# Loading and turning the first inputs of a fused attention and ELU-FFN kernel in another layout, with one block of M made early

## The chip, the cores and the metric

The kernel runs on one core of a Trainium2 chip. The metric is the device time of one execution in microseconds; a kernel's time is the median over its runs.

## The reference

`x` is (8, 8, 512, 64): batch B, heads H, tokens S, width D. `state` is (8, 8, 32, 64). Everything is fp32.

```python
scores = x @ state^T / 8;   xread = softmax(scores) @ state      # per batch and head, 512 x 32
scores2 = state @ x^T / 8;  sread = softmax(scores2) @ x         # 32 x 512
t = concat([xread, sread], axis=2)                               # 544 tokens per batch
t = t.transpose(0, 2, 1, 3).reshape(4352, 512)                   # heads side by side
h = t @ w_in                                                     # 512 -> 2048
g = where(h > 0, h, exp(min(h, 0)) - 1)
out = g @ w_out                                                  # 2048 -> 512
```

## The kernel before

**Algebra.** For the x part, xread @ w_in is a @ (state @ w_in): the kernel makes M = blockdiag(state) @ w_in for each batch (256 rows: 8 heads x 32 states) and multiplies the turned softmax `aT` with it (`ffn1_plain`, `ffn1_chunk`). w_in is cut into eight column blocks `hc` of 256; `make_m(b, hc)` makes one block of M with small products in PE tiles of 64 x 32 (`by_state`), and ACT copies it from PSUM. The 256 state tokens of all batches are read (`state_read`) batch by batch and put through the FFN at the end (`states`). Batches 2 to 7 use Strassen-Winograd sums for both FFN products, batches 0 and 1 for the second.

**Weights.** `convert` brings each weight block into another bit form with two ACT and four DVE passes. The eight w_in blocks and eight w_out blocks pass through three raw buffers (`t_w`), so block n + 3 is loaded when block n has been converted. A converted w_in block is also stored to DRAM (`w_in_mem`), and from batch 2 on `fetch(hc)` brings it back, 512 KB each.

**Stages.** `start()` does batches 0 and 1 together with the conversion of the weights: x of batch 0 is loaded and turned (`load_x`, `turn_x`), then scores, `softmax`, one block of M after another, FFN products as each is ready, the row softmax and the state read; then the w_out blocks and the second product. x of batch 0 lies in `xe` (`x_halves`), that of batch 1 in `g` (`x_1`). Then `ffn2_1` for batch 1 and `batch(b)` for 2 to 7, in which the first blocks of M of the next batch (`first_m`, `next_m`) and its softmax lie between the products of the running one; there x is loaded a second time in a blocked form and turned by DVE (`load_blocks`, `turn_blocks`), and the row softmax is brought in place by 16 small moves on SP's queue (`move_state`).

**Order.** Every operation is recorded in a `Plan` first. `ORDERS` holds one list of operation numbers for each engine, written out; `Plan.follow` walks through them with estimated costs (`DMA_COST`, `LAG`, `LANDING`), and by these picks PSUM banks, the interleaving in which instructions are emitted, and where PE gets fillers: products of the identity into a free bank while PE would wait, in the first 40 us of the plan. Nothing of the estimates acts on the chip but these choices. SP's queue issues nearly all transfers in its written order. All of this goes through helpers, so that in the profile nearly everything has line L525; fillers are L1675. Tiles tell the operations apart: `ps<-sec,xe` turns x of batch 0, `ps<-sec,g` that of batch 1, `ps<-o,kT` are the scores of batches 0 and 1, `ps<-w_half,kT` blocks of M, `ps<-aT,m` and `ps<-s,g` the first FFN products of batches 0 and 1, `ps<-xe,xr` a state read; `w_half<-t_w` and `t_w<-t_w` on ACT, `w_half` and `t_w` on DVE are conversions.

Of the kernel before, what the change touches and what calls it, by code (L numbers as in the profile page):

```python
# [11 lines left out]
FP32 = mybir.dt.float32  # L12
# [10 lines left out]
    "load_w": (0.44, 285e3), "load_w4": (0.44, 370e3), "load_x": (0.6, 270e3), "load_states": (0.6, 75e3),  # L23
    "load_blocks": (0.66, 280e3, 1.5), "move_state": (0.66, 280e3),
    "store": (0.44, 200e3), "store_q": (0.44, 90e3),
# [15 lines left out]
def in_order(text):  # L41

    ops = []
    for part in text.split():
# [40 lines left out]
    ),  # L85
    DVE: in_order(
# [152 lines left out]
class Plan:  # L239
# [6 lines left out]
        ACT: {PE: 0.23, DVE: 0.14, ACT: 0.12, POOL: 0.18, SP: 0.2},  # L246
        POOL: {PE: 0.12, DVE: 0.08, ACT: 0.08, POOL: 0.1, SP: 0.2},
    }
    LANDING = 2.2
    TURN = 0.1  # L250
    KEPT_BANKS = 0

# [107 lines left out]
    def follow(self, orders, until=0.0):  # L360
# [14 lines left out]
        def choice(op):  # L375
            if op.number < self.all_banks:
                return banks
# [1339 lines left out]
```

## Time and profile before

| | |
|---|---|
| time, median of 3 runs | 692.6 us (692.35 to 692.69) |
| span of the profiled execution | 689.9 us |
| outside the span, against the median | 2.7 us |
| PE busy (fillers included) | 683.8 us |
| DVE / ACT / GpSimd busy | 571.6 / 328.5 / 107.9 us |
| fillers on PE (L1675) up to 46 us | 16.7 us, 120 matmuls |
| bytes moved | 78.56 MB, of 111400 packets 89188 under 512 B |

The span runs from the first to the last instruction. An fp32 product is two matmuls in the trace, a transpose is one. "PEld" is the weight load of PE, which lies beside the matmuls. The durations of neighbouring matmuls overlap, so a step from start to start is the better measure of what one costs. A busy engine is not always doing needed work: fillers count as busy.

### The profile page before, as it was taken

How to read it: one execution, taken by the hardware profiler on the slowest of the kernel's cores; microseconds unless marked ns; L12 is line 12 of the kernel's file. 1: busy time of each engine (PE TensorE's matmuls, PEld its weight loads, DVE VectorE, ACT ScalarE, POOL GpSimd, SP SyncE). 2: the span in 40 equal slices, each digit the busy share in tenths (PEclk: the TensorE clock that was granted, in tenths of full speed). 3: DMA queues.
4: the chain of work that ended last, by engine and by line, in shares of the span. 5: the costliest groups of instructions: out<-in, count | busy, mean ns of one | idle time of the engine just before them, and what ended most of it. 6: DMA issues, size and time to landing. Idle time of an engine off the chain costs nothing.

```text
span 689.9 us, 14828 instructions
## 1 busy us (share of the span) xinstructions
PE 683.8 (99%) x5968; PEld 593.6 (86%) x5968; DVE 571.6 (83%) x897; ACT 328.5 (48%) x728; POOL 107.9 (16%) x133
## 2 busy tenths in 40 slices
PE   9999999999999999999999999999999999999997
PEld 7544568889988998899989998899889998999996
DVE  3999999989859994999679976998599966988661
ACT  4899973201268233842286316822383328611530
POOL 0200000110141115111240132212330333000000
PEclk9999999999999999999999999999999999999999
DMA  9767972003772237440383035232634030330401
GB/s 241 233 214 258 265 199 73 2 0 109 212 180 76 68 91 196 98 124 1 120 214 106 22 118 125 96 109 63 190 69 133 22 123 3 104 111 1 153 1 31
DMA packets 111400, 78.56 MB, mean 114 GB/s; under 512 B 89188, under 2 KB 92900, under 8 KB 111332
## 3 DMA queue, kind: packets, MB, share of 16 engines
q1 hardware_dynamic: 109120, 77.06, 39.1%
q8 instruction: 47, 0.77, 0.4%
q10 hardware_dynamic: 2212, 0.56, 0.4%
q14 instruction: 21, 0.17, 0.1%
HBM read 61.34 MB, written 13.11 MB: 108 GB/s over the span
## 4 chain that ended last, share of the span: by engine, by line
PE 96%; DVE 1%; ACT 1%; POOL 0%; issue 0%; POOLq 0%
PE ps L525 94%; PE ps L1675 2%; DVE sec L525 1%; ACT sec L525 0%; ACT o L525 0%; ACT w_half L525 0%; POOL sec L525 0%; ACT t_w L525 0%; ACT xr L525 0%; DVE s L525 0%; DVE w_half L525 0%; ACT g L525 0%; POOL sec masks.py:199 0%; DVE o L525 0%; ACT m L525 0%
## 5 line engine op out<-in xcount | busy, mean ns | idle before, releaser
L525 ACT COPY ps<-ps 128x128 f32<-128x128 f32 (+2 forms) x169 | 54.9, 331 | 228.2 <-PE ps L525 193.0
L525 PE MATMUL ps<-aT,m 128*128 128x256 f32 (+1 forms) x568 | 150.7, 406 | 0.1
L525 PEld LDWEIGHTS ps<-aT,m 128*128 128x128 f32 x568 | 104.3, 190 | 29.2 <-issue 11.6
L525 PE MATMUL ps<-w_out,g 128*128 128x128 f32 (+1 forms) x768 | 117.2, 293 | 0.0
L525 PEld LDWEIGHTS ps<-w_out,g 128*128 128x128 f32 x768 | 102.8, 192 | 6.6 <-issue 1.8
L525 DVE TENSOR_TENSOR o<-o,ps 128x256 f32<-128x256 f32 (+2 forms) x108 | 56.7, 533 | 38.1 <-PE ps L525 29.7
L525 POOL TENSOR_TENSOR m<-m 128x256 f32<-128x256 f32 x72 | 56.8, 807 | 134.4 <-ACT m L525 74.8
L525 PE MATMUL ps<-sec 128*128 128x128 f32 x560 | 72.7, 275 | 0.0
L525 POOL TENSOR_TENSOR xr<-xr,small 128x512 f32<-128x512 f32 x24 | 29.2, 1232 | 267.0 <-DVE small L525 146.9
L525 PE MATMUL ps<-t_w,s 128*128 128x128 f32 (+1 forms) x432 | 69.3, 299 | 0.0
L525 PEld LDWEIGHTS ps<-sec 128*128 128x128 f32 x560 | 67.7, 192 | 1.4 <-ACT ps L525 0.8
L525 PEld LDWEIGHTS ps<-t_w,s 128*128 128x128 f32 x432 | 59.0, 191 | 4.7 <-DVE sec L525 0.8
L525 ACT ACTIVATE xe<-ps 128x512 f32<-128x512 f32 x96 | 56.2, 599 | 11.5 <-PE ps L525 5.6
L525 DVE SCALAR_TENSOR_TENSOR g<-xe,ps 128x512 f32<-128x512 f32 x66 | 44.2, 681 | 6.8 <-ACT xe L525 6.4
L525 DVE TENSOR_TENSOR ps<-sec,ps 128x512 f32<-128x512 f32 (+1 forms) x52 | 34.8, 671 | 11.0 <-PE ps L525 7.1
L525 ACT COPY m<-ps 128x512 f32<-128x512 f32 (+1 forms) x56 | 29.2, 529 | 27.0 <-PE ps L525 27.0
L525 ACT ACTIVATE xe<-xe 128x512 f32<-128x512 f32 x66 | 41.1, 635 | 1.1
L525 PE MATMUL ps<-aT,s 128*128 128x256 f32 x168 | 41.2, 379 | 0.0
L525 ACT COPY sec<-ps 128x512 f32<-128x512 f32 (+1 forms) x52 | 29.6, 570 | 22.0 <-PE ps L525 21.8
L525 PE MATMUL ps<-w_out,sec 128*128 128x256 f32 (+1 forms) x176 | 38.5, 351 | 0.0
L525 PE MATMUL ps<-sec,g 128*128 128x128 f32 (+1 forms) x300 | 36.9, 270 | 0.0
L525 PEld LDWEIGHTS ps<-aT,s 128*128 128x128 f32 x168 | 31.9, 190 | 4.3
(148 smaller groups left out, 1165.9 us busy)
## 6 DMA issues: line engine op xcount, KB each, us to landing
w_half<-w_in_mem SPq DMA_DIRECT2D x54, 512.0 KB
t_w<-in_moe_w_out_dram SPq DMA_DIRECT2D x8, 1024.0 KB
t_w<-in_moe_w_in_dram SPq DMA_DIRECT2D x7, 1024.0 KB
out_dram<-o SPq DMA_DIRECT2D x14, 512.0 KB
xe<-in_x_dram SPq DMA_DIRECT2D x26, 256.0 KB
o<-in_x_dram SPq DMA_DIRECT2D x80, 64.0 KB
w_in_mem<-w_half SPq DMA_DIRECT2D x8, 512.0 KB
xr<-xr SPq DMA_DIRECT2D x96, 32.0 KB
```

Source lines behind the costliest of these rows:

```text
L525: ins = getattr(engine, name)(**named)
L1675: nc.tensor.matmul(psum[:, i, part * 256 : part * 256 + P], ident, rhs, start=not part, stop=True, skip_group_check=True,)
```

## The change

- `load_x` brings x of a batch in four DMAs by pairs of heads, in runs of 256 elements (1 KB: four tokens of a head), where it went in four DMAs by token residue in runs of 64 (256 bytes). All eight batches use it.
- `turn_x` turns x of batches 0 and 1 by products: each 64 x 64 block is the stationary operand and a 64 x 64 identity the moving one, in four PE tiles of 64 x 64. It took transposes of 64 x 128 blocks.
- The states come in four DMAs of 128 KB (two batches each, on 32 partitions) and are turned at the start, where 16 DMAs of 32 KB brought them, 12 of these later.
- In the first queues x of batch 0 leads, then the states of batches 0 and 1, then w_in's block 0, x of batch 1, the other states, blocks 1 and 2. It was block 0, state, x of batch 0, block 1, x of batch 1.
- `early_m` makes block 0 of M for batches 2 to 7 in the first weight step, into w_out's still unused space, and stores it in DRAM (`m_mem`). `first_m` then fetches that 256 KB block and makes one block (`make_one`) where it fetched 512 KB of w_in and made two.
- `load_blocks(2)` stands earlier in SP's order. In `start`, `y` takes any free bank. The estimates of the plan differ, fillers are spaced otherwise (21 are left of 60), and all five orders are new. Code lines move by 7 and more: helpers are L532, fillers L1731.

```diff
-    def load_x(b, to, queues=(SP,)):
-        x_v = x[b].rearrange("h (p r) d -> p r h d", r=R)
-        for r in range(R):
-            dma(x_rows(to, r).rearrange("p (h d) -> p h d", d=D), x_v[:, r], ...)
+        x_v = x[b].rearrange("(m g) (p r) d -> m p g (r d)", g=G, r=R)
+        for m in range(NP):
+            dma(x_pair(to, m).rearrange("p (g q) -> p g q", g=G), x_v[m], ...)
...
     def turn_x(at, to, both=False):
         for i in range(2):
             ps = [bank(), bank()]
-            for m in range(NP):
-                for r in range(2):
-                    calls += turn_calls(
-                        [v[t][:, m, r] for t in range(2)],
-                        x_rows(at, 2 * i + r)[:, m * P : (m + 1) * P],
-                    )
-            turns(0.6, calls, "turn_x")
+            for m in range(2):
+                for r in range(R):
+                    for g in range(G):
+                        for t in range(2):
+                            rows, d = slice(t * 64, (t + 1) * 64), slice(g * D, (g + 1) * D)
+                            calls.append((
+                                v[t][d, m, r], x_rows(at, 2 * i + m, g, r)[rows],
+                                ident[rows, rows],
+                                dict(start=True, stop=True, tile_position=(t * 64, g * D)),
+                            ))
+            products(1.03, calls, "turn_x", "turn_x")
...
+    def load_states(q, raw, queue=SP):
+        dma(
+            raw[q * NS : (q + 1) * NS].rearrange("p (k d) -> p k d", d=D), state_v[q],
+            queue=queue, kind="load_states",
+        )
+    def turn_states(qs, raw):
+        ps = [bank() for q in qs]
+        for k in range(2 * NP):
+            for q, p in zip(qs, ps):
+                rows = slice(q * NS, (q + 1) * NS)
+                calls.append((
+                    p[:, k * NS : (k + 1) * NS], raw[rows, k * P : (k + 1) * P],
+                    ident[rows, rows], dict(tile_position=(q * NS, 0)),
+                ))
...
+    early = w_out.rearrange("p h k q -> p (h k q)")[:, : B * 512].rearrange("p (b n) -> p b n", n=512)
+    def early_m():
+        w = st["w", 0]
+        for b in range(2, B, 2):
+            ps = [bank(), bank()]
+            calls = []
+            for i in range(2):
+                calls += by_state(b + i, ps, [w[:, m] for m in range(NP)],
+                                  slice(i * 256, (i + 1) * 256), i == 0)
+            products(0.92, calls, "make_m", "state")
+            for g in range(G):
+                A.copy(out=early[:, b : b + 2, g * 256 : (g + 1) * 256],
+                       in_=ps[g].rearrange("p (b q) -> p b q", b=2))
+        for b in range(2, B):
+            dma(m_mem[:, b], early[:, b], tokens=((), (f"early{b}",)), kind="keep_m")
+    def fetch_early(b):
+        dma(m_to[0][:, :1024].rearrange("p (g q) -> p g q", g=G)[:, :, :256],
+            m_mem[:, b].rearrange("p (g q) -> p g q", g=G),
+            tokens=((f"early{b}",), ()), kind="fetch_m")
+    def make_one(b, hc):
+        ps = st[b, "m", hc] = [bank(), bank()]
+        w = st["w", hc]
+        products(0.46, by_state(b, ps, [w[:, m] for m in range(NP)], slice(0, 256)), "make_m", "state")
...
-        load_states(0, 1, raw_s, q2)
+        load_states(0, raw_t)
         blocks[0] = weight_block(0, 2)
         load_x(0, x_halves, q2)
-        load_states(1, 2, raw_s[:, 1:], (SP,))
+        for q in range(1, 4):
+            load_states(q, raw_t)
         read_block(1)
         load_x(1, x_1)
         read_block(2)
...
+            make_m(1, hc)
             if hc == 0:
-                turn_states(raw_s[:, 1:2], kT[:, 1:2])
-            make_m(1, hc)
+                early_m()
...
-            y = fixed[o is n1].view().rearrange("p (h c) -> p h c", h=2)
+            y = o.open()
...
     def first_m(b, now=True):
-        fetch(0)
         fetch(1)
-        make_m(b, 0, 1)
-        copy_m(b, 0, m_to[0])
+        fetch_early(b)
+        make_one(b, 1)
+        copy_one(b, 1, m_to[0])
...
                 while at < until and t + 0.45 < at:
...
-                    t += 0.25
+                    t += 0.45 if t < 5.5 else 0.24
```

More of the change, by code (lines that the diff above doesn't have):

```diff
@@ L22 @@
 DMA_COST = {
-    "load_w": (0.44, 285e3), "load_w4": (0.44, 370e3), "load_x": (0.6, 270e3), "load_states": (0.6, 75e3),
-    "load_blocks": (0.66, 280e3, 1.5), "move_state": (0.66, 280e3),
-    "store": (0.44, 200e3), "store_q": (0.44, 90e3),
+    "load_w": (0.46, 325e3), "load_x": (0.55, 297e3, 0.2), "load_states": (0.6, 180e3, 0.2),
+    "load_blocks": (0.66, 280e3, 2.1), "move_state": (0.66, 280e3, 0.6),
+    "store": (0.44, 200e3, 0.6), "store_q": (0.44, 90e3, 0.6),
 }
@@ L248 @@
     }
-    LANDING = 2.2
+    LANDING = 1.6
     TURN = 0.1
@@ L352, in prepare @@
             self.kept.setdefault(b.first, []).append(b.fixed)
-        self.all_banks = min([op.number for op in self.kept], default=0)
+        first = min([op.number for op in self.kept], default=0)
+        self.nofix = {
+            op for op in self.ops
+            if op.number >= first or any(b.last.number >= first for b in self.opening.get(op, ()))
+        }
     def lag(self, a, b):
@@ L375, in choice @@
         def choice(op):
-            if op.number < self.all_banks:
+            if op not in self.nofix:
                 return banks
@@ L411, in follow @@
             if e == PE:
-                t = free_at[PE]
-                while at < until and t + 0.35 < at:
+                t = max(free_at[PE], 1.4)
+                while at < until and t + 0.45 < at:
                     free = [i for u, i in banks if u <= t]
@@ L482 @@
     w_out_v = moe_w_out.rearrange("(fo fi) c -> fi fo c", fi=P).bitcast(U32)
-    state_v = state.rearrange("b (m c) n d -> c m n b d", c=G)
+    state_v = state.rearrange("(q b) h n d -> q n (b h) d", b=2)
     w_in_mem = ctx.enter_context(
@@ L487 @@
     ).tile([P, 2 * FC, NP, 256], FP32, name="w_in_mem")
+    m_mem = ctx.enter_context(
+        tc.tile_pool(name="mem_m", bufs=1, space=bass.MemoryType.DRAM)
+    ).tile([P, B, 512], FP32, name="m_mem")
     psum = ctx.enter_context(tc.tile_pool(name="ps", bufs=1, space=PSUM)).tile(
@@ L550, in call @@
                     port = port or len(wide) > 1
+                    if name == "reciprocal":
+                        cost = 0.07 + 6.0 * n
                 elif self.key == ACT:
-                    cost = 0.055 + 0.84 * n
+                    apart = any(a.ap[-1][0] != 1 for a in wide)
+                    cost = 0.055 + (0.965 if apart else 0.84) * n + 0.04 * (n < 0.1)
                     cost += 0.1 * sum(k in kw and is_ap(kw[k]) for k in ("scale", "bias") if k in kw)
@@ L609, in dma @@
         engine = nc.sync if queue == SP else nc.scalar
-        cost, rate, *wait = DMA_COST.get(kind, (0.44, 370e3))
+        cost, rate, *wait = DMA_COST.get(kind, (0.44, 370e3, 0.6))
         op = plan.add(
@@ L640, in load_x, with x_pair, x_rows @@
     def load_x(b, to, queues=(SP,)):
-        x_v = x[b].rearrange("h (p r) d -> p r h d", r=R)
-        for r in range(R):
-            dma(
-                x_rows(to, r).rearrange("p (h d) -> p h d", d=D), x_v[:, r],
-                queue=queues[r % len(queues)], kind="load_x",
-            )
-    def x_rows(at, r):
-        return at[r // 2][:, r % 2 * DM : (r % 2 + 1) * DM]
+        x_v = x[b].rearrange("(m g) (p r) d -> m p g (r d)", g=G, r=R)
+        for m in range(NP):
+            dma(
+                x_pair(to, m).rearrange("p (g q) -> p g q", g=G), x_v[m],
+                queue=queues[m % len(queues)], kind="load_x",
+            )
+    def x_pair(at, m):
+        return at[m // 2][:, m % 2 * 512 : (m % 2 + 1) * 512]
+    def x_rows(at, m, g, r):
+        return x_pair(at, m)[:, (g * R + r) * D : (g * R + r + 1) * D]
     x_halves = [xe[:, i * 1024 : (i + 1) * 1024] for i in range(2)]
@@ L674, in turn_x @@
             ps = [bank(), bank()]
-            v = [p.rearrange("p (m r q) -> p m r q", m=NP, q=64) for p in ps]
+            v = [p.rearrange("p (m r q) -> p m r q", m=2, q=64) for p in ps]
             calls = []
-            for m in range(NP):
-                for r in range(2):
-                    calls += turn_calls(
-                        [v[t][:, m, r] for t in range(2)],
-                        x_rows(at, 2 * i + r)[:, m * P : (m + 1) * P],
-                    )
-            turns(0.6, calls, "turn_x")
+            for m in range(2):
[9 more added lines that the diff above has]
+            products(1.03, calls, "turn_x", "turn_x")
             o = to.rearrange("p (m r t q) -> p m r t q", m=NP, r=R, q=64)
@@ L686, in turn_x @@
                 (V.tensor_copy if both and t else A.copy)(
-                    out=o[:, :, 2 * i : 2 * i + 2, t], in_=v[t]
+                    out=o[:, 2 * i : 2 * i + 2, :, t], in_=v[t]
                 )
-    def load_states(b0, b1, raw, queues):
-        for b in range(b0, b1):
-            for c in range(G):
-                dma(
-                    raw[:, b - b0, c], state_v[c, :, :, b],
-                    queue=queues[c % len(queues)], kind="load_states",
-                )
-    def turn_states(raw, to):
-        ps = [bank(), bank()]
-        n = to.shape[1]
-        v = [p[:, : n * 64].rearrange("p (b q) -> p b q", q=64) for p in ps]
-        calls = []
-        for b in range(n):
-            calls += turn_calls(
-                [v[t][:, b] for t in range(2)], raw[:, b].rearrange("p c d -> p (c d)")
-            )
-        turns(0.07 * n + 0.05, calls, "turn_states")
-        o = to.rearrange("p b (t q) -> p t b q", t=2)
-        for t in range(2):
-            (V.tensor_copy, A.copy)[t](out=o[:, t], in_=v[t])
+    def load_states(q, raw, queue=SP):
[13 more added lines that the diff above has]
+                ))
+        turns(0.3 if len(qs) == 1 else 0.5, calls, "turn_states")
+        for q, p in zip(qs, ps):
+            if q:
+                (V.tensor_copy, A.copy)[q % 2](
+                    out=kT[:, 2 * q : 2 * q + 2],
+                    in_=p[:, : 2 * P].rearrange("p (b q) -> p b q", b=2),
+                )
+            else:
+                for b in range(2):
+                    (A.copy, V.tensor_copy)[b](out=kT[:, b], in_=p[:, b * P : (b + 1) * P])
     def by_state(b, ps, rhs, cols, start=True):
@@ L777, in copy_m @@
         g_of[b, c] = to
+    early = w_out.rearrange("p h k q -> p (h k q)")[:, : B * 512].rearrange(
+        "p (b n) -> p b n", n=512
+    )
+    def early_m():
+        w = st["w", 0]
+        for b in range(2, B, 2):
+            ps = [bank(), bank()]
+            calls = []
+            for i in range(2):
+                calls += by_state(
+                    b + i, ps, [w[:, m] for m in range(NP)], slice(i * 256, (i + 1) * 256), i == 0
+                )
+            products(0.92, calls, "make_m", "state")
+            for g in range(G):
+                A.copy(
+                    out=early[:, b : b + 2, g * 256 : (g + 1) * 256],
+                    in_=ps[g].rearrange("p (b q) -> p b q", b=2),
+                )
+        for b in range(2, B):
+            dma(m_mem[:, b], early[:, b], tokens=((), (f"early{b}",)), kind="keep_m")
+    def fetch_early(b):
+        dma(
+            m_to[0][:, :1024].rearrange("p (g q) -> p g q", g=G)[:, :, :256],
+            m_mem[:, b].rearrange("p (g q) -> p g q", g=G),
+            tokens=((f"early{b}",), ()), kind="fetch_m",
+        )
+    def make_one(b, hc):
+        ps = st[b, "m", hc] = [bank(), bank()]
+        w = st["w", hc]
+        calls = by_state(b, ps, [w[:, m] for m in range(NP)], slice(0, 256))
+        products(0.46, calls, "make_m", "state")
     def copy_m_half(b, hc, to):
@@ L894, in state_read @@
                         read_weights()[:, m, g, r],
-                        x_rows(at, r)[:, m * P + g * D : m * P + (g + 1) * D],
+                        x_rows(at, m, g, r),
                         dict(start=r == 0, stop=r == R - 1, tile_position=(0, m * NS)),
@@ L1247, in start @@
         g_flat = g_sb.rearrange("p k s -> p (k s)")
-        raw_s = g_flat[:, : 2 * P].rearrange("p (b c d) -> p b c d", b=2, c=G)
-        raw_t = xr[:, : 6 * P].rearrange("p (b c d) -> p b c d", b=6, c=G)
+        raw_t = xr[:, : 8 * P]
         m1 = [g_flat[:, (c + 1) * 2048 : (c + 1) * 2048 + 1024] for c in range(3)]
@@ L1276, in start @@
             op.rank = k
-        turn_states(raw_s[:, 0:1], kT[:, 0:1])
+        turn_states([0], raw_t)
+        turn_states([1, 2, 3], raw_t)
         def w_step(hc):
@@ L1320, in start @@
             convert_block(n)
-            if n == 9:
-                load_states(2, B, raw_t, (SP,))
-                turn_states(raw_t, kT[:, 2:B])
         A.copy(out=read(1), in_=read(1, True))
```

250 rows, old and new, of the table ORDERS are left out of this document.

## The prediction, made before the changed kernel had run

> **What bounds the kernel now.** I read the chain that ended last first, in two stretches, since its share of TensorE (96%) hides that the first 46 us and the rest have different limits.
>
> ```profile
> 1.36 9.30 PE ps L1675 x66
> ...
> 13.46 0.69 PE ps L525 x16
> 14.14 0.57 ACT o L525
> ...
> 16.89 1.25 DVE sec L525 x2
> ...
> 27.53 5.45 DVE sec L525 x9
> ...
> 36.43 9.25 PE ps L525 x112
> 45.68 0.13 issue
> 45.80 34.22 PE ps L525 x227
> ```
> ```profile
> 79.81 606.29 PE ps L525 x5250
> 686.10 0.02 issue
> ```
>
> From 45.80 to 686.10 us PE never stops: whatever is taken out of it there is gained in full, and nothing else counts. Ahead of that the chain goes through DVE, ACT and GpSimd. L1675 is the filler: products of the identity that fill PE's waits. The groups of lines up to 46 us give them
>
> ```profile
> L1675 PE MATMUL ps<-sec 128*128 128x128 f32 x120 | 16.7, 299 | 1.5 <-POOL sec masks.py:199 1.4 <-ACT o L525 0.2
> ```
>
> 60 products, so 16.7 us of PE's "work" is waiting in disguise. For what? The timeline: x of batch 0 is turned at 12.33 and 13.39, its scores start at 15.01, and DVE can start the softmax at 16.25:
>
> ```profile
> 13.39 0.71 PE L525 MATMUL ps<-sec,xe 64*128 64x64 f32 x16
> 15.01 1.09 PE L525 MATMUL ps<-o,kT 64*32 64x512 f32 x16 [0.31 <-DVE o L525]
> 16.25 1.31 DVE L525 STREAM_TRANSPOSE sec<-ps 128x512 f32<-128x512 f32 x2 [1.39 <-PE ps L525]
> ```
>
> From there the table by stretches shows the two feeders full (columns: PE, PEld, DVE, ACT, POOL):
>
> ```profile
> 26.00:36.00 10.00, 10.00 (x119) 5.02 (x120) 9.97 (x18) 9.88 (x22) 2.05 (x2) 1.00 0.66 208
> 36.00:46.00 10.00, 9.75 (x123) 4.67 (x129) 9.62 (x13) 9.92 (x21) 0.00 (x0) 1.00 0.51 165
> ```
>
> So an earlier x moves the start of a chain that DVE and ACT then carry to about 46 us (ACT to about 75), and the gain ends at whichever of PE, DVE, ACT gains least.
>
> **x of batch 0: loads.** The DMA view, one microsecond of 2 KB runs with few short ones, and one of 256-byte runs:
>
> ```profile
> DMA packets 230, 0.36 MB, mean 360 GB/s; under 512 B 60, under 2 KB 60, under 8 KB 230
> DMA packets 869, 0.22 MB, mean 217 GB/s; under 512 B 869, under 2 KB 869, under 8 KB 869
> ```
>
> Before, 1 MB of weights goes first and x0's 256-byte runs are through at about 10.3. Changed: x0 leads both queues. The first packets move at 1.9, and the first full microsecond loses 0.5 us (182 of 360 KB). 1 KB runs are in no row; 1 MB takes 2.9 us at the 2 KB rate, 4.7 at the 256-byte rate. Per engine a packet takes 18 ns at 256 bytes and 88 at 2 KB; a straight line gives 48 at 1 KB, 333 GB/s, 3.15 us, which I take (bounds -0.25, +1.55). Last packet to landing: the first weight half has its 256th packet at about 3.85 and ACT starts on it at 4.49, so 0.6. x0 lands at 1.9 + 0.5 + 3.15 + 0.6 = 6.15. The first four heads' states, 512 packets at 869 per us, land at 6.75. [...]
>
> **x: turning.** 16 transposes a group step 0.65. The replacement, 32 identity products (64 matmuls, 64 columns), is nearest to the state read, 64 matmuls of 64 columns in 1.03: four groups cost 4 x 0.38 = 1.5 us more. One group ends the path: 6.15 to 7.2; states turned by 7.5; copies of x on DVE and ACT to 8.0 (0.60 and 0.5); kT copies, ACT then DVE on one bank, to 8.5; scores 8.75 to 9.8; DVE starts at 10.0, against 16.25: **6.25 us earlier**.
>
> **What this is worth on each engine.** In the changed order w0's conversion (DVE 3.8, ACT 2.1) stands inside batch 0's softmax, where before it lay under the wait for x.
> - PE: DVE's queue from its first transpose to aT holds 12.15 us by rows (0.63 a transpose, 0.60 a 512 pass, 0.34 a clamp, 0.61 a custom step), so the first FFN product starts at 10.0 + 12.15 + 0.2 = 22.4, against 25.92. Behind it PE holds 653.9 us before, 650.8 changed (0.865 a product of 512 columns, 0.43 of 256, 0.223 of 128, 0.064 a state product; this sum is 0.7% short of the trace from 45.8 on). Gain 3.5 + 3.1 = 6.6.
> - DVE, at batch 1's turned softmax, the point where PE starved at 36.4: 20.1 us of queue before, 23.85 changed (+3.75), with 644.7 and 641.1 us of PE behind (-3.6). Gain 6.25 - 0.15 = 6.1.
> - ACT, from its first exponential (19.29; changed 13.04): w1's conversion (2.1) and the early copies (below, 3.4) come ahead, 5.5; PE behind 3.6 shorter. Bound by sums: before 684.2 to 684.8 (PE ended at 686.1, so up to 1.9 to spare), changed 686.2 - 6.25 = 679.95. Gain 6.1 if ACT never idles; it idled 0.6 between 19 and 75.
>
> Hence 6.1 - 0.6 = 5.5, less 0.3 for the sixth weight block (rival 1): **5.2 us**.
>
> **Early M.** 48 state products (3.1 us) move from the batches, where PE is full, to the start. In each of six batches 32 matmuls (1.03) become 16 (0.52): -3.1. It is a gain only because they run before the first FFN product, in time that is filler now; it is in PE's 3.1 above (5.0 us more done by then, less the 1.9 us that x and states add). ACT pays 6 x 0.57 = 3.4 at the start; the 0.5 saved per batch, with ACT 20 to 40% busy, is worth nothing. Bytes are even: 512 KB fetched per batch becomes 256 written, 256 read. Six stores, at the end of products, join SP's queue ahead of weight loads: rival 1. If PE were already full there, 3.1 of the gain would go.
>
> **Edits at nothing:** x of batches 2 to 7 (hidden, PE waits for no DMA there); 12 state loads of 32 KB leave SP's queue between 17 and 102 us and 384 KB go behind x1 (landing about 15.2, needed about 16); state transposes +0.4 us of PE, counted; a free bank for y; GpSimd's orders. Fillers fall from 60 to 21; cover is PE's waiting.
>
> **Rivals.**
> 1. *Weights late, gain 2 to 4, 689.6.* The weights now queue behind x and states. DVE's third instruction is w0's clamp, ahead of the score transposes: w0's first half lands at 8.2, and from 8.8 on each us costs one. Later, w6's load stands behind 1.5 MB of M and w_in stores; issued at 44, landing 50 to 51, wanted by ACT at 51.2. For it: ACT waited 1.44 us for a weight at 98.94 before. Against: no such wait in the first 75 us.
> 2. *Cold clock, gain 3.7, 688.9.* Fillers ran 7 matmuls in the stretch 4 to 5 us and 11 from 5 to 6, though the granted clock reads 1.00:
>
> ```profile
> 4.00:5.00 1.00, 1.00 (x7) 1.00 1.06 360
> 5.00:6.00 1.00, 1.00 (x11) 1.00 1.03 295
> ```
>
> Changed, seven fillers end at 3.5 and PE idles until x lands. If it stays slow, the last turn, states and scores (2.35 us) take 11/7 of that: +1.5. Against: all later PE work there has slack. [...]
>
> 3. *Slower, 694.6.* In each batch the fetch of early M (256 KB) goes between x and the state moves in SP's queue, and the state read on PE waits for the last move. At batch 2 the last move is issued 4.4 us ahead of the read, against 5.4 before; at later batches 6.0 to 6.4 against 7.1 to 8. Each us beyond that is a PE stall in a stretch that has none. Stalls of 1.2 us in all six batches (7.2) outweigh 5.2; it decides from 0.9 each. Against: such moves took under 5.4 before without a stall.
> 4. *No change, 692.6.* The start was never x's wait but DVE's and ACT's total. Against: DVE was idle from 13.9 to 16.25 but for one copy.
>
> **How the numbers follow.** The profiled execution has a span of 689.9; the median of the runs, 692.6, is 2.7 above it, launch and end outside the span. 689.9 - 5.2 = 684.7, and 687.4 on the runs' scale. Chances: forecast (gain 4.2 to 7) 0.59; rival 1 0.20; rival 2 0.09; rival 4 0.05; rival 3 0.07. Low end: x at the full rate and ACT without idle, gain 7: 685.6. High end: x at 217 GB/s with one of rivals 1 and 2, gain 2.2: 690.4. Beyond it lie rivals 3 and 4 and a little of rival 1. A measurement here tells apart 0.2%, 1.4 us: faster 0.88, same 0.05, slower 0.07.
>
> **What would show it.** Right: scores near 8.8, DVE's first transpose near 10, FFN products from about 22.4, a chain of PE alone from about 40, PE's dense end near 681, state products of 16 matmuls less per batch. Wrong: the first transpose after 11.5 (loads or clock); ACT or DVE waiting for a weight DMA before 75; PE idle after 60; a state read waiting for xr.

## The result, and the profile after

The changed kernel takes 688.93 us (688.23 to 689.86), the kernel before beside it 692.64: a ratio of 0.995, with a 95% interval of 0.9935 to 0.9964. A second measurement gave 0.9947 (0.9933 to 0.9961). So 3.5 to 3.7 us are gained, where 5.2 were forecast. The median span of its ten runs is 686.95 us; that of 74 runs of the kernel before is 690.5.

The start first: TensorE's timeline (start, us, engine, line, operation, tiles, shapes, count, idle before it).

```profile
4.64 1.32 PE L532 MATMUL ps<-sec,xe 64*64 64x64 f32 x64
6.32 1.16 PE L532 MATMUL ps<-sec,xe 64*64 64x64 f32 x64
...
8.58 1.09 PE L532 MATMUL ps<-o,kT 64*32 64x512 f32 x16
...
15.53 0.69 PE L532 MATMUL ps<-sec,g 64*64 64x64 f32 x32 [0.69 <-DMA g<-in_x_dram]
...
17.65 0.68 PE L532 MATMUL ps<-sec,xr 32*128 32x32 f32 x22 [0.39 <-DMA xr<-in_state_dram]
...
19.07 1.09 PE L532 MATMUL ps<-o,kT 64*32 64x512 f32 x16
19.95 2.37 PE L532 MATMUL ps<-w_half,kT 64*32 64x256 f32 x80
22.24 1.34 PE L532 MATMUL ps<-xe,xr 128*32 128x64 f32 x64
```

x of batch 0 is turned at 4.64 and 6.32 by the new products (before: 12.33 and 13.39), and its scores start at 8.58 (before: 15.01). Then the later loads show: x of batch 1 makes TensorE wait up to 15.53, the states up to 17.65, and batch 1's scores start only at 19.07. From there TensorE is full, and the first FFN product starts at 23.51 (before: 25.92). DVE's timeline beside it:

```profile
9.76 1.31 DVE L532 STREAM_TRANSPOSE sec<-ps 128x512 f32<-128x512 f32 x2
...
21.30 0.69 DVE L532 TENSOR_SCALAR w_half<-w_half 128x1024 f32<-128x1024 f32 x1 [0.69 <-ACT w_half L532]
21.91 0.70 DVE L532 STREAM_TRANSPOSE aT<-sec 128x512 f32<-128x512 f32 x1
```

The softmax starts at 9.76 and aT is complete at 22.61. The one hole, 0.69 us ahead of 21.30, is a wait for ACT, which itself had stood 0.65 us at 18.36 for the states that TensorE turns at 17.65. The chain that ended last has the late states, then ACT, and one more delay in batch 3:

```profile
2.24 6.41 DMA t_w<-in_moe_w_in_dram
8.66 8.94 DMA xr<-in_state_dram
17.65 1.26 PE ps L532 x26
...
25.53 0.60 ACT sec L532
...
70.29 136.16 PE ps L532 x893
...
249.74 5.47 DMA m<-m_mem
255.35 99.59 PE ps L532 x948
```

From 25.53 to 70.25 us the chain goes through ACT alone, where the prediction expected TensorE alone from about 40; TensorE is busy beside it but for 0.5 us. The last states land 8.94 us after their issue, although from 14 us on the DMA view shows only some 50 short packets a microsecond (below). Batch 3's fetch of early M is issued at 249.74, among that batch's state moves, lands 5.47 us later, and TensorE stands still 1.10 us for it at 255.35. This is the place in SP's queue of rival 3, as a wait of an FFN product instead of a state read.

### The profile page after: what moved, and what is told of

It reads as the page before. It is cut to its first block, busy times and chain, and to the rows that moved or that the text cites. A ratio compares the mean times of both kernels' runs of the same rounds, so it can differ in the third digit from the quotient of the medians.

```text
span 687.0 us, 15056 instructions
## 1 busy us (share of the span) xinstructions
PE 678.3 (99%) x6098; PEld 588.6 (86%) x6098; DVE 568.5 (83%) x896; ACT 328.7 (48%) x734; POOL 110.2 (16%) x133
## 4 chain that ended last, share of the span: by engine, by line
PE 71%; issue 7%; ACT 6%; DMA 5%; DVE 5%; SPq 4%; POOL 1%; DVEq 0%; POOLq 0%
PE ps L532 71%; SPq L532 4%; ACT sec L532 3%; DMA xr<-in_state_dram 1%; DVE g L532 1%; POOL xr L532 1%; DMA o<-in_x_dram 1%; ACT t_w L532 1%; DVE xr L532 1%; DMA t_w<-in_moe_w_in_dram 1%; ACT w_half L532 1%; DMA m<-m_mem 1%; DVE sec L532 1%; DMA out_dram<-o 1%; ACT w_out L532 1%
## 5 line engine op out<-in xcount | busy, mean ns | idle before, releaser
L532 ACT COPY ps<-ps 128x128 f32<-128x128 f32 (+2 forms) x169 | 55.3, 332 | 227.6 <-PE ps L532 170.2
L532 PE MATMUL ps<-aT,m 128*128 128x256 f32 (+1 forms) x568 | 149.1, 406 | 1.1 <-DMA m<-m_mem 1.1
L532 PEld LDWEIGHTS ps<-aT,m 128*128 128x128 f32 x568 | 105.0, 190 | 29.4 <-issue 11.7
L532 PE MATMUL ps<-w_out,g 128*128 128x128 f32 (+1 forms) x768 | 115.4, 293 | 0.0
L532 PEld LDWEIGHTS ps<-w_out,g 128*128 128x128 f32 x768 | 102.1, 192 | 6.2 <-ACT m L532 1.7
L532 DVE TENSOR_TENSOR o<-o,ps 128x256 f32<-128x256 f32 (+2 forms) x108 | 55.9, 531 | 39.2 <-PE ps L532 34.3
L532 POOL TENSOR_TENSOR m<-m 128x256 f32<-128x256 f32 x72 | 56.9, 805 | 120.3 <-ACT m L532 103.9
L532 POOL TENSOR_TENSOR xr<-xr,small 128x512 f32<-128x512 f32 x24 | 31.0, 1305 | 278.0 <-PE ps L532 168.5
L532 PE MATMUL ps<-sec 128*128 128x128 f32 x560 | 72.9, 276 | 0.0
L532 PEld LDWEIGHTS ps<-sec 128*128 128x128 f32 x560 | 67.7, 192 | 1.0 <-issue 0.4
L532 PE MATMUL ps<-t_w,s 128*128 128x128 f32 (+1 forms) x432 | 67.9, 299 | 0.0
L532 ACT ACTIVATE xe<-ps 128x512 f32<-128x512 f32 x96 | 55.5, 597 | 14.4 <-PE ps L532 8.0
L532 PEld LDWEIGHTS ps<-t_w,s 128*128 128x128 f32 x432 | 59.0, 191 | 3.8 <-issue 0.8
L532 DVE SCALAR_TENSOR_TENSOR g<-xe,ps 128x512 f32<-128x512 f32 x66 | 43.9, 678 | 7.3 <-ACT xe L532 6.8
L532 DVE TENSOR_TENSOR ps<-sec,ps 128x512 f32<-128x512 f32 (+1 forms) x52 | 34.7, 668 | 9.7 <-PE ps L532 6.3
L532 ACT ACTIVATE xe<-xe 128x512 f32<-128x512 f32 x66 | 41.0, 633 | 1.1
L532 PE MATMUL ps<-aT,s 128*128 128x256 f32 x168 | 41.1, 379 | 0.2 <-DVE ps L532 0.2
L532 ACT COPY sec<-ps 128x512 f32<-128x512 f32 (+1 forms) x52 | 29.6, 569 | 21.2 <-PE ps L532 21.1
L532 ACT COPY m<-ps 128x256 f32<-128x256 f32 (+1 forms) x56 | 26.9, 497 | 26.6 <-PE ps L532 26.3
L532 PE MATMUL ps<-sec,g 128*128 128x128 f32 (+1 forms) x392 | 37.7, 259 | 1.2 <-DMA g<-in_x_dram 1.2
L532 PEld LDWEIGHTS ps<-sec,g 128*128 128x128 f32 (+1 forms) x392 | 34.7, 173 | 2.5 <-DMA g<-in_x_dram 1.7
L532 PE MATMUL ps<-w_out,sec 128*128 128x256 f32 (+1 forms) x176 | 36.6, 351 | 0.0
```

The costliest lines, as they stand in the source:

```text
L532: ins = getattr(engine, name)(**named)
```

## The experiments

All kernels ran beside the kernel before; each is compared by its ratio to it. The changed kernel's two ratios average 0.9949, and 0.001 is 0.7 us. With intervals of about 0.0013 to either side, differences under 1 us between variants are not settled by the ratios alone. The plan places the fillers anew for each order, so a moved load can also change their number. Most edits move operations in the written orders by their numbers:

```diff
+def move(queue, ops, behind):
+    line = ORDERS[queue]
+    for op in ops:
+        line.remove(op)
+    at = line.index(behind) + 1
+    line[at:at] = ops
```

**Again, and the fetch earlier.** The first run is the changed kernel itself.

> The changed kernel once more, beside the three variants below: 688.9 us as measured before, span 687.0. If its stalls are the kernel's and not that one execution's, TensorE waits again about 1.1 us for the fetch of early M in batch 3 (near 255 us), and the first FFN product starts again near 23.5 us; if they were chance, neither is there and the span is near 685.

0.9947. The first FFN product started at 23.48. The wait for the fetch was 0.4 us this time, but ACT waited 1.34 us at 54.30 for the weight load issued at 44.97, which it had not in the first profile. So the stalls at the start belong to the kernel, and those on fetched and loaded blocks vary from one execution to the next.

```diff
+move(SP, [863], behind=869)     # batch 3's fetch of early M
```

> Only the fetch of batch 3's early M moves in SP's queue, to right behind the weight fetch ahead of it (near 216 us instead of 249.7). Theory (the fetch's place in the queue costs its stall): the wait of 1.1 us at 255 us is gone, every product behind it is 1.1 us earlier, and the time falls by 1.1 us against the changed kernel, to about 687.8. Rival (another engine is late there too, so the stall only changes its name): TensorE waits for M's copy or sums of batch 3 instead, and the time falls by less than 0.3 us. Second rival (traffic pushed aside): loads of batch 4's x blocks land later and cost what was won.

0.9941 (0.9927 to 0.9956); TensorE's wait for the fetch is gone from the profile, and nothing takes its place near 255 us. Once more:

> The kernel with only the earlier fetch of early M for batch 3, once more beside the others of this call: 687.9 us, a wait of 0.3 to 0.4 us at the state read of batch 4 (near 341 us) and none at 255 us.

0.9948 (0.9937 to 0.9960), and the wait at 255 us is again gone; the one expected near 341 us was not there this time. The mechanism is shown by the two profiles; that the time falls with it is not, since the two ratios lie 0.5 and 0.1 us below the changed kernel's.

**Three places, then two.**

```diff
+move(SP, [863], behind=869)
+move(SP, [170], behind=72)      # weight load ahead of three stores
+move(SP, [1360], behind=1289)   # output store behind batch 4's last state move
```

> The changed kernel with three places in SP's queue changed: batch 3's fetch of early M right behind the weight fetch ahead of it, the sixth-next weight load (issued at 45.0 us) ahead of three stores (1.25 MB), and the last state move of batch 4 ahead of an output store. Theory (each of these waits is a stall of TensorE or ACT): against the changed kernel 1.1 us for the fetch, 0 to 1.2 for the weight (ACT waited for it in one execution, not in the other), 0.3 to 0.5 for the move: 687.2 us, 0.5 below the kernel with the fetch alone. Rival (stalls reappear at the next landing): same as with the fetch alone, 687.9.

0.9975 (0.9962 to 0.9988): 1.8 us slower than the changed kernel. A stall did reappear at the next landing, as the rival said, but a larger one than either side priced. ACT's and TensorE's timelines and the chain of this kernel:

```profile
53.58 1.12 ACT L544 ACTIVATE w_half<-t_w 128x1024 f32<-128x1024 f32 x1 [2.51 <-DMA w_in_mem<-w_half]
```
```profile
55.11 3.46 PE L544 MATMUL ps<-s,g 128*128 128x512 f32 x4 [2.40 <-ACT g L544]
```
```profile
44.59 8.97 DMA w_in_mem<-w_half
```

The weight now landed in time, but the store of an earlier block, put behind it, took 8.97 us to land. The next conversion may overwrite that block only then, so ACT waited 2.51 us for the store and TensorE 2.40 for ACT. TensorE's granted clock then read 0.50 from 56 to 58 us.

```diff
+move(SP, [863], behind=869)
+move(SP, [1360], behind=1289)
```

> The changed kernel with two of the three places moved: batch 3's fetch of early M right behind the weight fetch ahead of it, and the last state moves of batch 4 ahead of an output store; the weight load of 45.0 us stays where it was. Theory (the weight load put ahead of the stores cost the kernel with three moves 2.4 us, since a store of a weight block then held up the next conversion): 1.1 us less than the changed kernel for the fetch and 0.4 to 0.8 for the move, so 687.1 to 687.4. Rival (the moves are worth nothing and the earlier gain was chance): 688.6, as the changed kernel.

0.9948 (0.9936 to 0.9960), the changed kernel's own ratio, though the waits at 255 and at 341 us are both gone. TensorE's long unbroken block started at 71.56 against 70.29 in the first profile of the changed kernel (and 71.73 in its second): the weight load again. No version here is shown to be faster than the changed kernel.

**Each part of the change undone.** First x in short runs: the layout has one row of all heads together, as before, so a run is 256 bytes.

```diff
-        x_v = x[b].rearrange("(m g) (p r) d -> m p g (r d)", g=G, r=R)
-        for m in range(NP):
+        x_v = x[b].rearrange("h (p r) d -> r p h d", r=R)
+        for r in range(R):
```

> x is read in 256-byte runs (one transfer for each of the four rows of a partition, as before) into the same tiles; identity products and order stay. By the rows before, 1 MB then takes 4.7 us instead of the 2.8 seen (364 to 384 GB/s), for x of batch 0 and again for x of batch 1. Theory (landing sets the start): x of batch 0 lands at about 8.4 instead of 6.5, DVE's first transpose starts near 11.6 instead of 9.8, x of batch 1 and the states land 3.8 us later, the first FFN product starts at 26 to 27 instead of 23.5, and the kernel is 2.0 to 3.5 us slower than the changed one. Rival (x was not what the start waits for, DVE's and ACT's queues are): first transpose late, but less than 0.7 us slower.

0.9999 (0.9984 to 1.0014): 3.5 us slower than the changed kernel, the upper end of what was expected. TensorE's timeline:

```profile
8.40 1.98 PE L532 MATMUL ps<-sec,xe 64*64 64x64 f32 x120 [1.20 <-DMA xe<-in_x_dram]
...
27.77 3.70 PE L532 MATMUL ps<-aT,m 128*128 128x512 f32 x8
```

x of batch 0 was complete at 8.40, the FFN started at 27.77, and TensorE's long block at 74.70 instead of 70.29. The granted clock read 0.51 from 18 to 20 us here, so a slow stretch of TensorE is in the 3.5 us too.

Next, weights first:

```diff
+move(SP, [5, 3, 0], behind=2)   # x and first states behind the weight's halves
```

> In SP's queue the first weight block's halves go ahead of SP's two loads of batch 0's x and the states of batches 0 and 1, as before; the other two loads of x stay first on ACT's queue. Theory (x first is worth its time on DVE): x lands at about 8.5 instead of 6.5, DVE's first transpose starts near 11.8, ACT's wait of 0.67 us for the weight's second half goes, and the first FFN product starts near 24.9; 1.2 to 2.0 us slower than the changed kernel. Rival (x of batch 1 and the states land when they did, and they set the first FFN product): less than 0.5 us slower.

1.0013 (1.0005 to 1.0022): 4.5 us slower than the changed kernel, more than either theory said. TensorE's timeline shows why:

```profile
1.36 7.59 PE L1741 MATMUL ps<-sec 128*128 128x128 f32 x44 [1.36 <-POOL sec masks.py:199]
8.88 2.12 PE L542 MATMUL ps<-sec,xe 64*64 64x64 f32 x128
10.93 0.68 PE L542 MATMUL ps<-sec,xr 32*128 32x32 f32 x8
11.54 0.49 PE L1741 MATMUL ps<-sec 128*128 128x128 f32 x2
11.96 1.09 PE L542 MATMUL ps<-o,kT 64*32 64x512 f32 x16
12.98 0.62 PE L542 MATMUL ps<-sec,g 64*64 64x64 f32 x25
16.16 2.67 PE L542 MATMUL ps<-sec,g 64*64 64x64 f32 x103 [2.56 <-issue]
```

Batch 0's scores start at 11.96 instead of 8.58, 3.4 us later where the theory had 2.0; since 44 fillers run until 8.95, x may have been there before. Then TensorE stands still for 2.56 us in the middle of turning batch 1's x, for nothing the profile records. Counted up, it stopped behind 44 + 128 + 8 + 2 + 16 + 25 = 223 matmuls. And the granted clock fell (third number from the end):

```profile
18.00:20.00 2.00, 2.00 (x37) 1.88 (x30) 2.00 (x5) 2.00 (x6) 0.00 (x0) 0.50 0.96 346
```

The FFN started at 28.77. So the 4.5 us are not the price of the order alone: the plan's 44 fillers, the pause and the slow clock are in them.

**x of batch 1 out of the way.** The same pause spoiled this one:

```diff
-        turn_x(x_1, ob)
+        turn_x(x_halves, ob)
+move(SP, [11, 12, 13, 14], behind=15)
```

> Batch 1's x is loaded behind the third weight block, and its turning takes batch 0's x in its place (the outputs of batch 1 are those of batch 0's x): nothing at the start waits for batch 1's x, and the states of batches 2 to 7 follow the first weights directly. Theory (the late landing of x of batch 1 and of the states sets the first FFN product): states land by about 13 instead of 17.6, scores of batch 1 start by 17.5 instead of 19.1, the first FFN product starts near 22.4 instead of 23.5, and the time falls by 0.8 to 1.2 us. Rival (from there on DVE's and ACT's total is the bound, and PE's late start is absorbed): the FFN starts earlier but PE waits that much more for ACT or DVE up to 75 us, and the time falls by less than 0.3 us.

0.996 (0.9948 to 0.9973): 0.8 us slower by the ratios, too little to be settled, where both theories said faster. Its timeline:

```profile
9.86 1.03 PE L542 MATMUL ps<-sec,xe 64*64 64x64 f32 x53
13.42 1.38 PE L542 MATMUL ps<-sec,xe 64*64 64x64 f32 x75 [2.53 <-issue]
...
18.49 0.62 PE L542 MATMUL ps<-sec,xr 32*128 32x32 f32 x21
19.90 0.25 PE L542 MATMUL ps<-sec,xr 32*128 32x32 f32 x3 [0.79 <-issue]
```

With nothing to wait for, TensorE came to its 223rd matmul at 10.9 and stood until 13.42; again at its 351st, 128 further on. So this run does not tell what the late x costs.

**Without early M.** Two ways: not made at all, or made and not used. In both, a batch makes its first block whole again. (In both, SP's queue has the fetch of the second weight block right behind the first. In the first kernel one choice of a PSUM bank is pinned as well, and operations are renumbered.)

```diff
-            if hc == 0:
-                early_m()              # this line pair in the first kernel only
...
-        fetch(1)
-        fetch_early(b)
-        make_one(b, 1)
-        copy_one(b, 1, m_to[0])
+        fetch(0)
+        fetch(1)
+        make_m(b, 0, 1)
+        copy_m(b, 0, m_to[0])
```

> Without early M: each batch makes its first block of M from a fetched weight block as the kernel before did, so 48 state products (3.1 us) go back from the start to the batches, six stores and ACT's 3.4 us of copies leave the start, and the fetch of early M, with its 1.1 us wait at batch 3, goes. Theory (the products are a gain of 3.1 since they run in time that is filler otherwise): +3.1 - 1.1 - up to 0.7 at the start = 1.3 to 2.0 us slower than the changed kernel. Rival (ACT is what the start waits for, and early M's copies cost there what they bring later): same or faster, 0 to -1.5 us.

0.9978 (0.9967 to 0.9988): 2.0 us slower than the changed kernel. TensorE's timeline, and its table by stretches (TensorE's granted clock is the third number from the end):

```profile
17.59 0.55 PE L553 MATMUL ps<-sec,sec 128*128 128x128 f32 x3
19.39 0.48 PE L553 MATMUL ps<-sec,sec 128*128 128x128 f32 x1 [1.26 <-issue]
...
20.23 1.96 PE L553 MATMUL ps<-o,kT 64*32 64x512 f32 x16
```
```profile
18.00:20.00 2.00, 0.74 (x5) 0.61 (x3) 2.00 (x5) 0.65 (x3) 0.00 (x0) 0.68 1.06 406
20.00:22.00 2.00, 2.00 (x26) 0.51 (x33) 0.54 (x3) 1.81 (x3) 0.00 (x0) 0.50 1.01 394
```

It stopped behind its 351st matmul too, and the clock then fell to 0.50: scores that take 1.09 us took 1.96. Its four runs with a mean clock of 0.995 or 0.996 average 691.7 us, the other eight 690.4. So part of the 2.0 us is this pause and not early M.

> Early M is made, copied and stored at the start as in the changed kernel, but no batch fetches it: each makes its first block of M whole from two fetched weight blocks, so the start is unchanged and each batch 2 to 7 has 16 state products more. Theory (TensorE is full from 80 us on): 6 x 0.52 = 3.1 us more in the batches, less the 1.1 us wait for the fetch of early M at batch 3, so 2.0 us slower than the changed kernel and 3.1 slower than the one with the earlier fetch. Rival (the products' cost was partly hidden): less than 1 us slower. If so much is lost and the kernel without early M lost less, the rest is what early M costs at the start.

0.9986 (0.9974 to 0.9998): 2.6 us slower than the changed kernel, where the theory had 2.0, and 2.9 slower than the two measurements of the earlier fetch, where it had 3.1; the rival's limit of 1 is left behind. The start is that of the changed kernel (FFN at 23.33), so this is the cleaner of the two, but not quite clean. TensorE has a new wait in batch 3:

```profile
285.48 0.70 PE L546 MATMUL ps<-aT,s 128*128 128x256 f32 x2 [1.52 <-ACT sec L546]
```

Behind it stands a late load of x blocks, for which DVE waited 1.9 us; their place in SP's queue is changed against the fetches. The groups of state products tell the products' own cost, of the changed kernel and of this one:

```profile
L532 PE MATMUL ps<-w_half,kT 64*32 64x256 f32 x1024 | 34.1, 381 | 0.5 <-ACT m L532 0.5
```
```profile
L546 PE MATMUL ps<-w_half,kT 64*32 64x256 f32 x1120 | 36.6, 380 | 0.7 <-ACT m L546 0.7
```

96 matmuls more take 2.5 us of TensorE's busy time.

**Fillers.** As dense as before, then none.

```diff
-                t = max(free_at[PE], 1.4)
-                while at < until and t + 0.45 < at:
+                t = free_at[PE]
+                while at < until and t + 0.35 < at:
...
-                    t += 0.45 if t < 5.5 else 0.24
+                    t += 0.25
```

> Fillers as densely as before the change (one in 0.25 us, from the first moment), so some 40 more of them run by 20 us. First theory (TensorE's clock is not open when x lands): turning of batch 0's x and its scores get faster, DVE's first transpose starts up to 0.4 us earlier, and the kernel gains up to 0.4 us. Second theory (TensorE's instructions come in 16 KB packets of about 128 matmuls with their weight loads; in two runs it stood still right behind its 223rd matmul and in two behind its 351st, with no wait the profile shows): with more fillers it reaches its 223rd matmul before the packet is there and stands still once more, 1 to 2.5 us somewhere between 10 and 14 us, and again at the 351st; x of batch 1 lands at 12.7 to 15.5 anyway, so the first FFN product moves by 0 to 1 us and the time by 0 to +1 us.

0.9998 (0.9987 to 1.0009): 3.4 us slower than the changed kernel; both theories were far too low.

```profile
1.36 5.77 PE L1731 MATMUL ps<-sec 128*128 128x128 f32 x32 [1.36 <-POOL sec masks.py:199]
7.05 1.16 PE L532 MATMUL ps<-sec,xe 64*64 64x64 f32 x64
...
18.50 0.25 PE L532 MATMUL ps<-sec,xr 32*128 32x32 f32 x3
20.69 0.62 PE L532 MATMUL ps<-sec,xr 32*128 32x32 f32 x21 [1.93 <-issue]
```

32 filler matmuls stand ahead of the first turn in TensorE's order and run until 7.13, while without fillers x could be turned from 4.57 (below): x waits for the fillers. Against the changed kernel's 4.64 that is 2.4 us; behind the 351st matmul a pause of 1.93 us follows (the second theory named that place; at the 223rd there was none). DVE's first transpose came at 12.31.

```diff
-    steps, fills = plan.follow(ORDERS, 40.0)
+    steps, fills = plan.follow(ORDERS, 0.0)
```

> No fillers at all; TensorE idles wherever it waits at the start. Theory (the granted clock closes without work, and a closed clock at the start costs what rival 2 of the prediction said): turning of x, states and scores of batch 0 take about twice as long as in the changed kernel (1.2 us a group of x), DVE's first transpose starts 2 to 3 us later, the granted clock reads about 0.5 up to some 4 us after the last long gap, and the kernel is 2 to 3.5 us slower than the changed one. Rival (x of batch 1, the states and DVE set the start whatever TensorE's speed): under 1 us slower. The instructions come sooner relative to need, so no stall behind the 223rd or 351st matmul.

0.996 (0.9946 to 0.9975): 0.8 us slower by the ratios, not settled, and within the rival's limit of 1; the theory's 2 to 3.5 is excluded. TensorE's first line, and stretches:

```profile
4.57 3.69 PE L532 MATMUL ps<-sec,xe 64*64 64x64 f32 x128 [4.57 <-DMA xe<-in_x_dram]
```
```profile
14.00:16.00 2.00, 1.06 (x52) 0.92 (x52) 2.00 (x5) 2.00 (x7) 0.64 (x1) 0.83 1.07 243
16.00:18.00 2.00, 2.00 (x40) 1.55 (x34) 2.00 (x5) 2.00 (x7) 0.00 (x0) 0.50 1.02 341
20.00:22.00 2.00, 2.00 (x32) 0.63 (x24) 1.46 (x4) 1.69 (x3) 0.00 (x0) 0.50 0.31 115
```

Turning x took 3.69 us instead of 2.48 in two groups, DVE started at 10.52 instead of 9.76, and the clock was at 0.50 from about 15 to 22 us, after TensorE had been idle for 2.0 of the 4 us from 10 to 14. The FFN started at 25.06, 1.5 us late.

## Why the prediction was right, and where it was not

- **x of batch 0.** Forecast to land at 6.15; its last pair was turned from 6.32, in the second profile from 6.02. (48 ns for 1,024 bytes on each of sixteen engines are 341 GB/s; the prediction wrote 333.) The one-kilobyte runs moved faster still; the DMA view of the microsecond from 4 to 5, and of two late ones, from 14 to 15 and 15 to 16:

```profile
DMA packets 393, 0.38 MB, mean 384 GB/s; under 512 B 18, under 2 KB 393, under 8 KB 393
DMA packets 146, 0.20 MB, mean 205 GB/s; under 512 B 51, under 2 KB 53, under 8 KB 146
DMA packets 209, 0.33 MB, mean 331 GB/s; under 512 B 54, under 2 KB 54, under 8 KB 209
```

  384 GB/s is above the 2 KB row of the kernel before (360). The "full rate" of the prediction's low end is that row's 2.9 us for 1 MB; that it is a limit no run shows. With short runs the same load was 2 us later (above).
- **Turning.** 1.16 us a group against the 1.03 of the state read, 1.32 for the first. The path absorbed it: scores 8.58 (forecast 8.75), first transpose 9.76 (forecast 10.0).
- **DVE's queue of 12.15 us to aT.** It took 22.61 - 9.76 = 12.85, and 0.69 of that is the wait for ACT: without it 12.16.
- **First FFN product, 22.4: it started at 23.51, and here a step failed.** The prediction listed the 384 KB of states under "edits at nothing", landing at 15.2 for a need at 16. They landed at 17.6. That delays batch 1's scores, and behind these stand 80 state products and the state read in TensorE's queue: 19.07 + 0.88 + 2.29 + 1.27, start to start, is 23.51. The prediction took DVE's aT for the last thing to be ready, and did not add up that queue. In the second run of the earlier fetch the states were there at 16.55, scores began at 17.96, and the FFN began 5.26 us later; without a pause of 0.76 us in the state read that would have been about 22.46 (an estimate).
- **Early M, 3.1 us.** The 96 matmuls more take 2.5 us in the groups. Not using it cost 2.6 us in time, about what 2.5 for the products, 1.5 for the new wait and the 0.4 to 1.1 won back at the fetch come to (2.9 to 3.6), within the error. So the gain is there, and somewhat smaller than 48 state products (two matmuls each) at the prediction's 0.064 made it.
- **TensorE's work behind the first FFN product, 3.1 us less.** This term was too large too. From that product to TensorE's last matmul (stretch, its length, busy time), before and after:

```profile
25.92:686.08 660.16, 659.91 (x5708) 1.00 0.38 109
23.51:683.34 659.83, 657.82 (x5587) 1.00 0.38 110
```

  The work is 2.1 us less. (The prediction had 653.9 and 650.8; both sums were some 1% short, as it said of the first.)
- **The fetch of early M** was priced at nothing unless state reads waited. It cost one wait of 1.1 us in the first profile, 0.4 in the second. Rival 3 had the right queue, but one stall in one batch, not six.
- **Rival 1, the sixth weight block.** 0.3 us were taken off for it. In one of two profiles ACT waited 1.34 us for it, in the other not. It was wanted at about the time named; its landing varied. The first block, which the rival also named, cost ACT a wait of 0.67 us at 10.03, for its second half.
- **Rival 2, the cold clock.** It did not happen in the changed kernel: the granted clock stayed at 1.00. Without any filler x was turned slowly (3.69 us against 2.48) and the clock fell later (0.50 from 16 to 22 us); the FFN started 1.5 us late and the ratios give 0.8 us, which is not settled. The measured 688.93 is rival 2's own 688.9, and that is chance.
- **Fillers at nothing.** Right for the change as it stands, but the cost of the opposite was not seen: with the old spacing 3.4 us of the 3.6 gained are lost.
- **2.7 us outside the span.** It is 1.8: the profiled execution of the kernel before (span 689.9) was 0.6 below its runs' median of 690.5.
- **The sum.** The time lies in the stated range, but the gain of 3.5 to 3.7 is below the band of 4.2 to 7 that the forecast gave itself and in rival 1's of 2 to 4, whose weight wait came in one of two profiles. TensorE's row had 3.5 + 3.1 = 6.6; the forecast took 5.2, since DVE's and ACT's rows gave 6.1 and waits took off 0.9. Measured in the first profiles: the first FFN product 2.4 us earlier (25.92 to 23.51), 2.1 less work behind it, and 1.75 more idle time, of which 1.10 is the fetch and 0.5 ACT. That gives the 2.7 us by which TensorE's last matmul came earlier (686.08 to 683.34). The span fell by 2.9 in these two profiles and by 3.55 on medians, since the profiled execution before was a quick one. So the states, the price of early M's products and the waits share what is missing.
- **Does a late FFN start reach the end?** It does. In the variants whose batches use early M the first FFN product started between 23.2 and 28.8 us, and from there to TensorE's last matmul it took 658.7 to 660.9 us in all of them (662.0 in the kernel with three moves and its wait of 2.40). A later start was not absorbed. Whether an earlier one would be kept in full is not shown, since ACT is busy without a break of more than 0.13 us from 18.4 to 70 us.
- **The signs.** Of the signs of being right, the scores, the first transpose and the smaller groups of state products came. TensorE alone from about 40 us (it was 70.29) and its end near 681 (683.3) did not. Of the signs of being wrong three came, all small: ACT waiting for a weight (0.67 and 1.34 us), TensorE idle after 60 us (1.10), and in the second profile a state read that waited 0.34 us for `xr`.

The parts do not add up to the whole. Undoing the long runs costs 3.5, the order 4.5, the filler spacing 3.4, early M's use 2.6 us, a wait of its own included: together nearly four times the gain. The first three have a stretch with the clock near 0.50 in them that the changed kernel has not, and two of them a pause of TensorE. In these runs an early x needed all three: with short packets, with weights ahead of it, or with fillers ahead of it in TensorE's queue it was turned late again.

## What to carry to other kernels

When a load is brought forward, look at what stands behind it in every queue that it passes: the transfers it pushes back (here states that nobody costed), and filler work that was sized for the old wait. A wait that goes by a changed place in a DMA queue is worth a run before it is counted: moving one load ahead of three stores made the stores the wait. And where single waits vary by 1 us from execution to execution, two profiles tell more than one.

## What the runs showed of the hardware

TensorE stood still, with no wait that the profile can name, behind the same count of matmuls in different kernels: 223 in two, 351 in three, and 478 of those recorded in the second run of the earlier fetch (a few records can be missing). The steps are 128 matmuls apart, each with its weight load. The records of the transfers have, in the queue marked "instruction", single packets of 16 KB: 48 of them with 0.79 MB in the changed kernel, whose 6098 recorded matmuls are 127 for each. In the kernel with x of batch 1 out of the way one of them comes between 10.3 and 12 us and takes 1.4 us, the next between 16 and 20 us and takes 1.2, and TensorE goes on at 13.42 and 19.90. With weights first one of 1.3 us comes between 12 and 16 us, and TensorE goes on at 16.16. The DMA view of 10 to 12 us in the kernel with x of batch 1 out of the way (4.3% of sixteen engines' 2 us are the 1.4 us):

```profile
DMA packets 966, 0.49 MB, mean 245 GB/s; under 512 B 834, under 2 KB 834, under 8 KB 965
...
q8 instruction: 1, 0.02, 4.3%
```

That TensorE waited for these packets, which share the DMA engines with the loads, is inferred from the counts and from these three pauses, and was not tested by itself. If it is so, many small matmuls at a start that is full of loads have a price that no group of the profile shows.

The granted clock fell to 0.50 or near it in six of the variants' profiles: with short runs (0.51 from 18 to 20 us), with weights first (0.50 from 18 to 20), with three moves (0.50 from 56 to 58), without early M (0.50 from 20 to 24), with the old fillers (0.62 from 22 to 24, 0.52 from 24 to 26) and without fillers (0.50 from 16 to 22). Their mean clocks over the span are 0.997, 0.998, 0.998, 0.995, 0.998 and 0.995. In each, TensorE had stood idle shortly before; in the same order, for 0.53 and 1.04 us, 2.56, 2.40, 0.42 and 1.26, 1.93, and without fillers for 2.0 of the four from 10 to 14. That the idle time made the clock fall is inferred from these six. Of the two pauses of 2.5 us one was followed by it (weights first), the other not (x of batch 1 out of the way, with the column at 1.00 up to 30 us); what makes the difference is not shown. In the first microseconds the column can't be relied on: the trace has no record of the clock before 5.05 us in the changed kernel, and the column counts that as 1.00. Without fillers x is turned from 4.57 to 8.26 at two thirds of the changed kernel's speed (3.69 us against 2.48), with 1.00 in the column.

Last, the late tail of the states. The 256-byte packets of the kernel before ran at 869 a microsecond over sixteen engines, 54 for one engine. The last ones of the states ran at 51 and 54 a microsecond from 14 to 16 us, then 19 and 9, beside weight traffic: it looks as if one engine was late with its share, and the landing at 17.6 with it. Two instruction packets of 1.1 and 1.4 us, at 9.8 and 14.0 us, would explain most of the 2.4 us by which the states missed the forecast; that they ran on that engine is not shown.
